# Down products of the second pair of chunks as 2x2 blocks of seven products, one stage behind each gate-up product

## The chip, the core and the metric

One core of a Trainium2 chip runs the whole program. Its engines are TensorE (PE, matrix products; its weight loads are shown as PEld), VectorE (DVE), ScalarE (ACT), GpSimd (POOL) and SyncE (SP, which issues transfers). Each engine runs its own instructions in order; semaphores make one engine wait for another. The metric is device time in microseconds (us), the median of the runs.

## What is computed

One transformer block on 2048 tokens of width 512, in float32: a linear-attention layer with adaptive layer norm, then a gated bilinear layer. The change touches only the second half of the latter, `h @ w_down`.

```python
h = _layernorm(x, axis=-1) * (1 + cb) + sb
g = jnp.einsum("bsd,df->bsf", h, w_gate)      # F = 1376
u = jnp.einsum("bsd,df->bsf", h, w_up)
x = x + gb * jnp.einsum("bsf,fd->bsd", g * u, w_down)
```

## The kernel before

Tokens are cut into four chunks of 512, each chunk into four token tiles of 128. F is cut into eleven f tiles: ten of 128 and number 10 of 96. To keep float32 accuracy on the fast float32r path of PE, every operand is split in a high part (an ACT cast, `split` L182-184) and a low part (a DVE or POOL subtraction, same helper), and every product is three: high by high, high by low, low by high.

**Gate and up.** Two chunks are treated together, (0, 1) first and (2, 3) second. For each f tile, `block` (L910) makes gate and up for both chunks as a 2x2 block product in seven products instead of eight (the Winograd form of Strassen's scheme). Its seven steps p1, p5, p6, p2, p7, p3, p4 are six PE products of 512 columns each (`times`, L887), into four PSUM banks a, b, c, d. Between them ACT copies banks on (`copy`, L896: a to b after p1, d to SBUF after p5, b to c and to SBUF after p6), and DVE adds and multiplies, so that after p3 and p4 the two tiles of h = gate x up are there, one for each chunk. `block` is a generator: it yields after each step, and callbacks in a table `at` put other work behind a step. These carry the preparation of coming weights: scaling of the down rows by `gb` (DVE, at p6), loads for one f tile ahead of the down rows and two ahead of gate/up (SP, at p7), casts and low parts of the gate/up weights of the next f tile (ACT and POOL, `Right.high` and `Right.lows`, at p7), split of the down rows (at p3), and differences of gate/up weights (POOL, `Right.sums`, at p4). The split of the two h tiles goes out at the start of the next block (`flush`).

**Down.** The second pair's f tiles are in groups (10, 0, 1), (2, 3, 4), (5, 6, 7), (8, 9). When a group's h tiles are ready, `down_group` (L964) multiplies them with the down rows, 128 tokens by 512 columns, three PE products for each f tile, token tile and chunk, all f tiles of a group summed in one PSUM bank of the four in the pool `ps_acc`. `evac` (L722) adds the bank to x on DVE and, in a chunk's last group, stores x. The groups' products are cut in parts (`cut_at`, L1064), and one part goes out behind each following block, in one run on PE (L1059-1063); those left over come behind the last block (L1068-1071), where the last token tile is made in two halves of 256 columns.

Of the kernel before, what the change touches and what calls it, by code (L numbers as in the profile page):

```python
# [9 lines left out]
F32R = mybir.dt.float32r  # L10
# [4 lines left out]
P = 128  # L15
# [7 lines left out]
def tile_adaln_block(  # L23
# [875 lines left out]
    def split_h(x, n):  # L899
        h, l = B("kh", dt=F32R)[:n], B("kl", dt=F32R)[:n]  # L900
        split(x, h, l)
        return h, l
# [4 lines left out]
        while todo:  # L907
            todo.pop(0)()

    def block(A, R, out, at, aside=False):  # L910


        n, R = R.n, R.of
        a, b, c, d = (x[:n] for x in banks)

        def T2(tag):
            return B(tag)[:n]

# [92 lines left out]

    draws = {}

    def draw_load(n):
        if n < len(steps):
            f0, k = fts[steps[n][1]]
            draws[n] = load(w_down[f0:f0 + k, :], "raw")

    trickle = []

# [6 lines left out]
    free = [False]  # L1027
    parts = []

    def ffn():  # L1030

        first_side, second_side = side, {}
        m = 0
        for g, (cs, fs) in enumerate(groups):
            last = g + 1 == len(groups) or groups[g + 1][0] != cs
            outs, ds = [], []
            A = first_side if cs == (0, 1) else second_side
            for f in fs:
                out = []
                draw = draws.pop(m)  # L1040

                def scale(d=draw):
                    nc.vector.tensor_tensor(d, d, gb[:d.shape[0]], op=ALU.mult)

                at = {"p6": [scale],
                      "p7": [lambda: draw_load(m + 1), lambda: right_load(m + 2), lambda: right_split(m + 1)],
                      "p3": [lambda: ds.append(split_raw(draw, low=nc.gpsimd))],
                      "p4": [lambda: right_sums(m + 2)]}
                for point in ("p1", "p5", "p6", "p3", "p4")[2 if m == 2 else 0:]:
                    at.setdefault(point, []).append(lambda: some(some_at.get(m, 0)))  # L1050
                if m + 1 < len(steps) and steps[m + 1][0] != cs:
                    at["p1"].append(lambda: fetch(stash, second_side, "a11", "s1"))
                    at["p7"].insert(0, lambda: fetch(stash, second_side, "s2", "a12", "s3"))
                elif m and steps[m - 1][0] != cs:
                    at["p1"].append(lambda: fetch(stash, second_side, "s4", "a22"))
                outs.append(out)
                yield from block(A, rights[m], out, at, aside=not free[0])
# [6 lines left out]
            cut_at = {2: ([[0, 1, 2, 3], []], [[], [0, 1, 2, 3]]),  # L1064
                      3: ([[0, 1, 2], []], [[3], [0, 1]], [[], [2, 3]])}[len((groups + groups[-1:])[g + 1][1])]
# [199 lines left out]
```

## Time and profile before

| | |
|---|---|
| median of 3 runs | 566.18 us (565.63 to 566.36) |
| the profiled execution | 565.84 us |
| its span, first to last instruction | 564.1 us |
| mean granted TensorE clock | 0.999 |
| eleven blocks of the second pair and what follows | from about 384 us to the end |

The profile's page shows the span with the busy time of each engine, the chain of work that ended last, and groups of equal instructions with their count, busy time, mean duration and the idle time in front of them with what ended it. Consecutive instructions of an engine overlap, PE's most of all, so that the time of a run of them is read from their starts. In a timeline each row has the start, the time, the engine, the line, operation, tiles and the count; square brackets show how long the engine sat idle and what released it.

### The profile page before, as it was taken

How to read it: one execution, taken by the hardware profiler on the slowest of the kernel's cores; microseconds unless marked ns; L12 is line 12 of the kernel's file. 1: busy time of each engine (PE TensorE's matmuls, PEld its weight loads, DVE VectorE, ACT ScalarE, POOL GpSimd, SP SyncE). 2: the span in 40 equal slices, each digit the busy share in tenths (PEclk: the TensorE clock that was granted, in tenths of full speed). 3: DMA queues.
4: the chain of work that ended last, by engine and by line, in shares of the span. 5: the costliest groups of instructions: out<-in, count | busy, mean ns of one | idle time of the engine just before them, and what ended most of it. 6: DMA issues, size and time to landing. Idle time of an engine off the chain costs nothing.

```text
span 564.1 us, 7356 instructions
## 1 busy us (share of the span) xinstructions
PE 556.8 (99%) x2568; PEld 457.1 (81%) x2568; DVE 377.4 (67%) x622; ACT 278.5 (49%) x499; POOL 187.0 (33%) x192
## 2 busy tenths in 40 slices
PE   7999999999999999999999999999999999999997
PEld 6788888888888778878878888887888888888886
DVE  7996968868869876759768877756444444344445
ACT  3695866446556546355875454534333333334120
POOL 2000000000011300000598756555667446446200
PEclk9999999999999999999999999999999999999999
DMA  8900224202301001804408363599336022200004
GB/s 286 380 5 2 74 76 131 94 0 72 83 2 57 19 1 38 260 0 150 131 2 295 116 206 112 184 350 310 113 112 189 17 57 56 57 19 2 0 1 149
DMA packets 50309, 59.34 MB, mean 105 GB/s; under 512 B 6432, under 2 KB 27168, under 8 KB 50272
## 3 DMA queue, kind: packets, MB, share of 16 engines
q1 hardware_dynamic: 50272, 58.87, 32.8%
q8 instruction: 20, 0.33, 0.2%
q14 instruction: 17, 0.14, 0.1%
HBM read 43.12 MB, written 15.73 MB: 104 GB/s over the span
## 4 chain that ended last, share of the span: by engine, by line
PE 92%; ACT 2%; DVE 2%; POOL 1%; issue 1%; DMA 1%; SPq 0%; POOLq 0%
PE bank L892 28%; PE acc L972 6%; PE acc L973 6%; PE acc L974 6%; PE acc L662 6%; PE bank L196 5%; PE bank L198 5%; PE bank L197 5%; PE acc L325 3%; PE acc L323 3%; PE acc L324 3%; PE bank L741 2%; PE bank L739 2%; PE bank L740 2%; PE bank L246 2%; PE bank L626 1%
## 5 line engine op out<-in xcount | busy, mean ns | idle before, releaser
L892 PE MATMUL bank<-h,w 128*128 128x512 f32 (+1 forms) x798 | 184.6, 390 | 0.0
L892 PEld LDWEIGHTS bank<-h,w 128*128 128x128 f32 (+1 forms) x798 | 148.4, 186 | 32.4
L897 ACT ACTIVATE bank<-bank 128x512 f32<-128x512 f32 (+1 forms) x38 | 22.1, 582 | 142.9 <-PE bank L892 142.9
L726 DVE TENSOR_TENSOR x<-acc,x 128x512 f32<-128x512 f32 (+1 forms) x73 | 48.9, 683 | 47.5 <-PE acc L974 46.7
L878 POOL TENSOR_TENSOR w<-raw,w 128x256 fp32r<-128x256 f32 (+3 forms) x38 | 42.4, 1115 | 103.0 <-ACT w L871 76.1
L184 POOL TENSOR_TENSOR w<-raw,w 128x512 fp32r<-128x512 f32 (+1 forms) x25 | 34.9, 1401 | 116.0 <-DVE mv L216 87.5
L972 PE MATMUL acc<-w,kh 128*128 128x512 f32 (+2 forms) x154 | 59.6, 387 | 0.0
L973 PE MATMUL acc<-w,kh 128*128 128x512 f32 (+2 forms) x154 | 59.6, 387 | 0.0
L974 PE MATMUL acc<-w,kl 128*128 128x512 f32 (+2 forms) x154 | 59.5, 386 | 0.0
L224 POOL TENSOR_TENSOR rstd<-ve,half 128x4 f32<-128x4 f32 (+1 forms) x10 | 10.6, 1061 | 123.2 <-DVE ve L223 121.6
L184 DVE TENSOR_TENSOR kl<-u,kh 128x512 fp32r<-128x512 f32 (+1 forms) x38 | 27.4, 761 | 31.8 <-ACT kh L183 28.0
L878 POOL TENSOR_TENSOR w<-t,w 128x512 fp32r<-128x512 f32 (+1 forms) x38 | 48.4, 1296 | 0.0
L196 PE MATMUL bank<-w,h 128*128 128x512 f32 x104 | 41.7, 401 | 0.0
L198 PE MATMUL bank<-w,h 128*128 128x512 f32 x104 | 40.6, 390 | 0.0
L197 PE MATMUL bank<-w,h 128*128 128x512 f32 x104 | 40.5, 389 | 0.0
L662 PE MATMUL acc<-w,xh 128*128 128x512 f32 x120 | 38.1, 399 | 0.0
L972 PEld LDWEIGHTS acc<-w,kh 128*128 128x128 f32 (+1 forms) x154 | 28.9, 188 | 6.0
L974 PEld LDWEIGHTS acc<-w,kl 128*128 128x128 f32 (+1 forms) x154 | 28.9, 188 | 5.9
L973 PEld LDWEIGHTS acc<-w,kh 128*128 128x128 f32 (+1 forms) x154 | 28.9, 188 | 5.9
L951 DVE TENSOR_TENSOR u<-bank,u 128x512 f32<-128x512 f32 (+1 forms) x19 | 13.1, 692 | 30.3 <-PE bank L892 26.8
L233 ACT ACTIVATE n<-x,nmr,rstd 128x512 f32<-128x512 f32 x30 | 22.7, 804 | 16.0 <-DVE nmr L227 16.0
L183 ACT ACTIVATE w<-raw 128x512 fp32r<-128x512 f32 (+2 forms) x44 | 26.2, 619 | 2.8 <-DMA raw<-in_A_wqkv_dram 1.9
(188 smaller groups left out, 1108.8 us busy)
## 6 DMA issues: line engine op xcount, KB each, us to landing
raw<-in_w_mod_dram SPq DMA_DIRECT2D x24, 256.0 KB, 3.8
raw<-in_B_w_down_dram SPq DMA_DIRECT2D x20, 256.0 KB, 3.4
raw<-in_B_w_gate_dram SPq DMA_DIRECT2D x36, 128.0 KB, 3.9
raw<-in_B_w_up_dram SPq DMA_DIRECT2D x36, 128.0 KB, 3.9
x<-in_A_x_dram SPq DMA_DIRECT2D x16, 256.0 KB, 5.8
kept<-f SPq DMA_DIRECT2D x16, 256.0 KB, 2.0
f<-kept SPq DMA_DIRECT2D x16, 256.0 KB, 4.3
side_s<-h SPq DMA_DIRECT2D x16, 256.0 KB, 2.5
```

What stands on the lines that cost most here:

```text
L183: nc.scalar.activation(h, src, AF.Copy)
L184: (low or nc.vector).tensor_tensor(l, src, f32(h), op=ALU.subtract)
L196: nc.tensor.matmul(ps, ah, bh, start=i == 0, stop=False)
L197: nc.tensor.matmul(ps, ah, bl, start=False, stop=False)
L198: nc.tensor.matmul(ps, al, bh, start=False, stop=i == n - 1)
L662: nc.tensor.matmul(yps[i], x, y, start=False, stop=k == KD - 1 and x is al, skip_group_check=True)
L726: nc.vector.tensor_tensor(xt[:, a:b], dn[j][:, a:b], xt[:, a:b], op=ALU.add)
L878: sub = lambda out, x, y: (on or nc.gpsimd).tensor_tensor(out, x, f32(y), op=ALU.subtract)
L892: mm = lambda x, y, **kw: nc.tensor.matmul(ps, x[:, k], y, skip_group_check=True, **kw)
L972: nc.tensor.matmul(ps, hh[:, a:b], dh[:n, c:d], start=i == 0, stop=False)
L973: nc.tensor.matmul(ps, hh[:, a:b], dl[:n, c:d], start=False, stop=False)
L974: nc.tensor.matmul(ps, hl[:, a:b], dh[:n, c:d], start=False, stop=i == len(hs) - 1)
```

## The change

The blocks of gate and up stay as they are. In the second pair, the down products of f tiles 0 to 7 are taken in pairs of f tiles, and each pair as a 2x2 block product by the same scheme: rows are the two chunks, inner blocks the two f tiles, columns the two halves of 256 output columns. A new class `Quad` holds one pair. Its left blocks are the four h tiles and four sums of them (DVE, `sum`; `split` makes high and low parts), its right blocks the quarters of the scaled down rows and four differences (POOL, `sums`), with four casts (ACT, `high`) and four low parts (POOL, `lows`).

`stages` makes the seven products for two token tiles at a time: six PE products of 256 columns per stage. It uses three of the four banks of `ps_acc` for the whole time: one bank for each token tile (its two halves hold p1 with p2 and p5 with p3) and a third whose halves are seeded with copies of p1 (ACT) and collect p6, p7 and p4. DVE adds to x after p5, p6, p7, p3 and p4. A pair has fourteen stages; each is put behind one gate-up product, and they run from the second step of the block two f tiles after the pair's first one.

The callbacks of a pair are spread over three blocks: scaling at p6 and p2 and the differences at p3 of the first; the split of a11, then s3, its split, the casts and the low parts at p1 and p5 of the second; s1, s2, s4 and the remaining splits at p1 to p7 of the third, in which the pair's stages begin and the next pair's scaling and differences stand as well. F tiles 10, 8 and 9 keep the plain down products, all behind the last block. The first pair of chunks is computed as before.

```diff
-    def block(A, R, out, at, aside=False):
+    def block(A, R, take_h, at, aside=False):
...
         def mul(ps, x):
             nc.vector.tensor_tensor(x, ps, x, op=ALU.mult)
-            todo.append(lambda: out.append(split_h(x, n)))
+            take_h(x, n)
...
+    class Quad:
+        DH = D // 2
+        ORDER = ("p1", "p5", "p6", "p2", "p7", "p3", "p4")
+        TERMS = {"p1": ("a11", "b11"), "p5": ("s1", "t1"), "p6": ("s2", "t2"), "p2": ("a12", "b21"),
+                 "p7": ("s3", "t3"), "p3": ("s4", "b22"), "p4": ("a22", "t4")}
+        SUMS = {"s1": ("a21", "a22", ALU.add), "s2": ("s1", "a11", ALU.subtract),
+                "s3": ("a11", "a21", ALU.subtract), "s4": ("a12", "s2", ALU.subtract)}
+        def __init__(self, cs):
+            self.cs = cs
+            self.h, self.left, self.right = {}, {}, {}
+            self.raws = []
+            self.names = ["a11", "a21", "a12", "a22"]
+        def take(self, x, n):
+            self.h[self.names.pop(0)] = x
+        def sum(self, n):
+            x, y, alu = self.SUMS[n]
+            self.h[n] = B("s")
+            nc.vector.tensor_tensor(self.h[n], self.h[x], self.h[y], op=alu)
+        def split(self, *names):
+            for n in names:
+                self.left[n] = split_h(self.h[n], P)
+        def sums(self):
+            d1, d2 = (d.rearrange("p (c n) -> p c n", c=2) for d in self.raws)
+            sub = lambda out, x, y: nc.gpsimd.tensor_tensor(out, x, y, op=ALU.subtract)
+            self.t12, self.t34 = (B("t", (P, 2, self.DH)) for _ in range(2))
+            sub(self.t12[:, 0], d1[:, 1], d1[:, 0])
+            sub(self.t12[:, 1], d2[:, 1], self.t12[:, 0])
+            sub(self.t34[:, 0], d2[:, 1], d1[:, 1])
+            sub(self.t34[:, 1], d2[:, 0], self.t12[:, 1])
+        def high(self):
+            d1, d2 = (d.rearrange("p (c n) -> p c n", c=2) for d in self.raws)
+            self.b11 = B("w", (P, 2, self.DH), F32R)
+            nc.scalar.activation(self.b11[:, 0], d1[:, 0], AF.Copy)
+            self.parts = []
+            for names, x in ((("t1", "t2"), self.t12), (("b21", "b22"), d2), (("t3", "t4"), self.t34)):
+                h = B("w", (P, 2, self.DH), F32R)
+                nc.scalar.activation(h, x, AF.Copy)
+                self.parts.append((names, x, h))
+        def lows(self):
+            sub = lambda out, x, y: nc.gpsimd.tensor_tensor(out, x, f32(y), op=ALU.subtract)
+            d1 = self.raws[0].rearrange("p (c n) -> p c n", c=2)
+            self.right["b11"] = (self.b11[:, 0], self.b11[:, 1])
+            sub(self.b11[:, 1], d1[:, 0], self.b11[:, 0])
+            for names, x, h in self.parts:
+                l = B("w", (P, 2, self.DH), F32R)
+                sub(l, x, h)
+                for i, n in enumerate(names):
+                    self.right[n] = (h[:, i], l[:, i])
+        def mm(self, ps, name, j, fresh=False):
+            left, right = self.TERMS[name]
+            (ah, al), (bh, bl) = (tuple(x[:, j * P:(j + 1) * P] for x in self.left[left]), self.right[right])
+            for n, (x, y) in enumerate(((ah, bh), (ah, bl), (al, bh))):
+                nc.tensor.matmul(ps, x, y, start=fresh and n == 0, stop=n == 2, skip_group_check=True)
+        def stages(self, own, seeded, js):
+            N = self.DH
+            x0, x1 = ([xts[c][j] for j in js] for c in self.cs)
+            def add(x, ps):
+                nc.vector.tensor_tensor(x, ps, x, op=ALU.add)
+            for name in self.ORDER:
+                for i, j in enumerate(js):
+                    u, d = own[i][:, :N], own[i][:, N:]
+                    self.mm({"p1": u, "p2": u, "p5": d, "p3": d}.get(name, seeded[i]), name, j, name == "p1")
+                for i, j in enumerate(js):
+                    if name == "p1":
+                        copy(seeded[i], own[i][:, :N])
+                    elif name == "p5":
+                        add(x1[i][:, N:], own[i][:, N:])
+                    elif name == "p6":
+                        add(x0[i][:, N:], seeded[i])
+                    elif name == "p7":
+                        add(x1[i][:, N:], seeded[i])
+                    elif name == "p3":
+                        add(x0[i], own[i])
+                    elif name == "p4":
+                        add(x1[i][:, :N], seeded[i])
+                yield
+        def run(self, banks):
+            own, seed = banks[:2], banks[2]
+            N = self.DH
+            for js in ((0, 1), (2, 3)):
+                yield from self.stages(own, (seed[:, :N], seed[:, N:]), js)
...
-    groups += [((2, 3), g) for g in ((10, 0, 1), (2, 3, 4), (5, 6, 7), (8, 9))]
     steps = [(cs, f) for cs, g in groups for f in g]
+    tail = (10, 8, 9)
+    steps += [((2, 3), f) for f in (10, 0, 1, 2, 3, 4, 5, 6, 7, 8, 9)]
+    M2 = len(steps) - 11
...
+    def plain_h(out):
+        return lambda x, n: todo.append(lambda: out.append(split_h(x, n)))
...
+    def scaled(d):
+        nc.vector.tensor_tensor(d, d, gb[:d.shape[0]], op=ALU.mult)
+    def plain_down(m, at, ds):
+        draw = draws.pop(m)
+        at["p6"].insert(0, lambda: scaled(draw))
+        at["p3"].insert(0, lambda: ds.append(split_raw(draw, low=nc.gpsimd)))
...
+        cs = (2, 3)
+        tail_h, tail_d = [], []
+        hold, running = [], []
+        quads = {}
+        late = {}
+        for n in range(4):
+            quads[m + 1 + 2 * n] = Quad(cs)
+        def advance():
+            while running and next(running[0], True):
+                running.pop(0)
...
+            if f in tail:
+                out = []
+                tail_h.append(out)
+                plain_down(m, at, tail_d)
+                take_h = plain_h(out)
+            elif m in quads:
+                q = quads[m]
+                take_h = q.take
+                for point in ("p6", "p2"):
+                    at[point].append(lambda n=point == "p2": scaled(q.raws[n]))
+                at["p3"].append(q.sums)
+                late[m + 1] = {"p1": [lambda q=q: q.split("a11")],
+                               "p5": [lambda q=q: q.sum("s3"), lambda q=q: q.split("s3"), q.high, q.lows]}
+                late[m + 2] = {"p1": [lambda q=q: q.sum("s1"), lambda q=q: q.split("s1")],
+                               "p5": [lambda q=q: q.sum("s2"), lambda q=q: q.split("s2")],
+                               "p6": [lambda q=q: q.split("a12"), lambda q=q: q.sum("s4")],
+                               "p2": [lambda q=q: q.split("s4")],
+                               "p7": [lambda q=q: q.split("a22")]}
+            if m + 1 in quads:
+                q1 = quads[m + 1]
+                at["p7"].insert(0, lambda: q1.raws.extend(draw_of(n) for n in (m + 1, m + 2)))
+            elif m + 1 < len(steps) and steps[m + 1][1] in tail:
+                at["p7"].insert(0, lambda: draw_load(m + 1))
+            if m - 2 in quads:
+                if not hold:
+                    hold.extend(acc_bank() for _ in range(3))
+                    nc.tensor.matmul(hold[2], wp[0][0][:, :P], wp[0][0], start=True, stop=True)
+                fresh = quads[m - 2].run(hold)
+            for n, _ in enumerate(block(second_side, rights[m], take_h, at)):
+                if n == 1 and m - 2 in quads:
+                    running.append(fresh)
+                advance()
+                yield
+            m += 1
+            if parts:
+                takes = [down_group(*p) for p in parts.pop(0)]
+                yield
+                for take in takes:
+                    take()
         flush()
-        while parts:
-            group = parts.pop(0)
-            for p in group:
-                down_group(*p, by_tile=not parts, end=not parts and p is group[-1])()
+        while running:
+            advance()
+        hold.clear()
+        for i, ch in enumerate(cs):
+            down_group(ch, i, [0, 1, 2, 3], tail_h, tail_d, True, by_tile=True, end=ch == cs[-1])()
```

More of the change, by code (lines that the diff above doesn't have):

```diff
@@ L1012, in tile_adaln_block, with draw_of @@
     draws = {}
+    def draw_of(n):
+        f0, k = fts[steps[n][1]]
+        return load(w_down[f0:f0 + k, :], "raw")
     def draw_load(n):
-        if n < len(steps):
-            f0, k = fts[steps[n][1]]
-            draws[n] = load(w_down[f0:f0 + k, :], "raw")
+        draws[n] = draw_of(n)
     trickle = []
@@ L1028, in tile_adaln_block, with base_points @@
     parts = []
+    def plain_h(out):
+        return lambda x, n: todo.append(lambda: out.append(split_h(x, n)))
+    def base_points(m):
+        cs = steps[m][0]
+        at = {p: [] for p in ("p1", "p5", "p6", "p2", "p7", "p3", "p4")}
+        at["p7"] += [lambda: right_load(m + 2), lambda: right_split(m + 1)]
+        at["p4"].append(lambda: right_sums(m + 2))
+        for point in ("p1", "p5", "p6", "p3", "p4")[2 if m == 2 else 0:]:
+            at[point].append(lambda: some(some_at.get(m, 0)))
+        if m + 1 < len(steps) and steps[m + 1][0] != cs:
+            at["p1"].append(lambda: fetch(stash, second_side, "a11", "s1"))
+            at["p7"].insert(0, lambda: fetch(stash, second_side, "s2", "a12", "s3"))
+        elif m and steps[m - 1][0] != cs:
+            at["p1"].append(lambda: fetch(stash, second_side, "s4", "a22"))
+        return at
@@ L1030, in ffn @@
+    def scaled(d):
[4 more added lines that the diff above has]
+        at["p3"].insert(0, lambda: ds.append(split_raw(draw, low=nc.gpsimd)))
+    second_side = {}
     def ffn():
-        first_side, second_side = side, {}
         m = 0
         for g, (cs, fs) in enumerate(groups):
-            last = g + 1 == len(groups) or groups[g + 1][0] != cs
+            last = g + 1 == len(groups)
@@ L1036, in ffn @@
             outs, ds = [], []
-            A = first_side if cs == (0, 1) else second_side
             for f in fs:
                 out = []
[L1040 to L1055, printed above, removed]
+                at = base_points(m)
@@ L1056, in ffn @@
+                plain_down(m, at, ds)
+                at["p7"].insert(1 if m == M2 - 1 else 0, lambda: draw_load(m + 1))
                 outs.append(out)
-                yield from block(A, rights[m], out, at, aside=not free[0])
+                yield from block(side, rights[m], plain_h(out), at, aside=not free[0])
                 m += 1
@@ L1063, in ffn @@
                         take()
-            cut_at = {2: ([[0, 1, 2, 3], []], [[], [0, 1, 2, 3]]),
-                      3: ([[0, 1, 2], []], [[3], [0, 1]], [[], [2, 3]])}[len((groups + groups[-1:])[g + 1][1])]
+            cut_at = ([[0, 1, 2], []], [[3], [0, 1]], [[], [2, 3]]) if last else ([[0, 1, 2, 3], []], [[], [0, 1, 2, 3]])
             parts.extend([(ch, i, js, outs, ds, last) for i, (ch, js) in enumerate(zip(cs, jss)) if js] for jss in cut_at)
-        flush()
-        while parts:
-            group = parts.pop(0)
-            for p in group:
-                down_group(*p, by_tile=not parts, end=not parts and p is group[-1])()
+        cs = (2, 3)
@@ new lines, in ffn @@
+        tail_h, tail_d = [], []
[7 more added lines that the diff above has]
+                running.pop(0)
+        while m < len(steps):
+            f = steps[m][1]
+            at = base_points(m)
+            for point, dos in late.pop(m, {}).items():
+                at[point] = dos + at[point]
+            if f in tail:
[37 more added lines that the diff above has]
+                    take()
```

## The prediction

> **What bounds the kernel now.** I read the page's busy shares and its chain first, then busy time by stretch, then the timeline of each engine in the second pair of chunks.
>
> ```profile
> PE 556.8 (99%) x2568; PEld 457.1 (81%) x2568; DVE 377.4 (67%) x622; ACT 278.5 (49%) x499; POOL 187.0 (33%) x192
> PE 92%; ACT 2%; DVE 2%; POOL 1%; issue 1%; DMA 1%; SPq 0%; POOLq 0%
> ...
> PE acc L143 <- DVE w L138: 2.0, 1, 2.0
> ...
> core 0: us, PE busy (x) PEld busy (x) DVE busy (x) ACT busy (x) POOL busy (x), PEclk, DMA share, GB/s
> 421.00:541.00 120.00, 120.00 (x530) 99.26 (x529) 51.73 (x80) 42.89 (x84) 63.48 (x66) 1.00 0.17 47
> ```
>
> PE is busy throughout and 92% of the chain; its longest wait is 2.0 us, at the start. In the 120 us where the second pair runs, PE never stops, at full granted clock, while DVE is at 43%, ACT 36%, POOL 53%, DMA 17%. Fewer PE columns are worth their whole time here, as long as nothing makes PE wait.
>
> **PE's own price.** Busy overlaps, so I count starts.
>
> ```profile
> 364.11 0.39 PE L972 MATMUL acc<-w,kh 128*128 128x512 f32 x1
> ...
> 369.55 9.68 PE L892 MATMUL bank<-h,w 128*128 128x512 f32 x42
> 379.07 0.39 PE L972 MATMUL acc<-w,kh 128*128 128x512 f32 x1
> ...
> 558.95 0.28 PE L972 MATMUL acc<-w,kh 128*128 128x256 f32 x1
> ...
> 560.02 0.28 PE L972 MATMUL acc<-w,kh 128*128 128x256 f32 x1
> ```
>
> Twenty-four down products of 512 columns take 369.55 - 364.11 = 5.44, 0.227 each; the 42 of a gate-up block 9.52. The tail has the new shape already: nine starts of 256 columns in 1.07, 0.119 each, 5% over half. Removed: 8 f tiles x 24 x 0.227 = 43.5. Added: 4 pairs x 7 stages x 4 token tiles x 3 = 336 x 0.119 = 40.0, a product that opens the third bank (0.2), and about 0.03 because the split last token tile now sums three f tiles. PE alone: **-3.3 us**. The work after PE's last product (add, store) is unchanged.
>
> **What is put beside PE.** The rows for each kind:
>
> ```profile
> L726 DVE TENSOR_TENSOR x<-acc,x 128x512 f32<-128x512 f32 x22 | 15.1, 692 | 28.2 <-PE acc L974 28.2
> L726 DVE TENSOR_TENSOR x<-acc,x 128x256 f32<-128x256 f32 x2 | 0.8, 425 | 0.3 <-PE acc L974 0.3
> 547.59 2.73 DVE L726 TENSOR_TENSOR x<-acc,x 128x512 f32<-128x512 f32 x4 [5.40 <-PE acc L974]
> 534.59 1.29 DVE L184 TENSOR_TENSOR kl<-u,kh 128x512 fp32r<-128x512 f32 x2 [1.95 <-ACT kh L183]
> 535.80 0.68 DVE L1043 TENSOR_TENSOR raw<-raw,row 128x512 f32<-128x512 f32 x1
> L183 ACT ACTIVATE kh<-u 128x512 fp32r<-128x512 f32 x16 | 9.1, 622 | 0.0
> 399.90 0.58 ACT L897 ACTIVATE bank<-bank 128x512 f32<-128x512 f32 x1 [7.01 <-PE bank L892]
> 402.57 0.58 ACT L897 ACTIVATE bank<-bank 128x512 f32<-128x512 f32 x1 [0.55 <-PE bank L892]
> 403.06 0.59 ACT L897 ACTIVATE u<-bank 128x512 f32<-128x512 f32 x1
> 403.54 0.42 ACT L871 ACTIVATE w<-raw 128x256 fp32r<-128x256 f32 x1
> 403.85 1.15 ACT L874 ACTIVATE w<-t 128x512 fp32r<-128x512 f32 x2
> 404.89 0.63 ACT L874 ACTIVATE w<-raw 128x512 fp32r<-128x512 f32 x1
> L878 POOL TENSOR_TENSOR w<-t,w 128x512 fp32r<-128x512 f32 x14 | 17.8, 1293 | 0.0
> L878 POOL TENSOR_TENSOR w<-raw,w 128x256 fp32r<-128x256 f32 x7 | 5.2, 737 | 41.8 <-ACT w L871 41.8
> L860 POOL TENSOR_TENSOR t<-raw,raw 128x256 f32<-128x256 f32 x7 | 5.2, 738 | 0.0
> ```
>
> Consecutive instructions overlap: starts lie 0.68 apart for a DVE add out of PSUM, 0.61 for a DVE operation in SBUF, 0.49 for an ACT copy out of PSUM, 0.52 for a cast of 512, 0.31 for one of 256; a dependent instruction of another engine sees the full duration (0.69, 0.63, 0.42). An ACT copy of 256 columns out of PSUM isn't shown: between 0.31 and 0.49 I take 0.31, its width's row.
>
> Per pair of f tiles (two blocks, about 29 us) DVE gains 16 adds of 256 (0.43) and 4 of 512, 4 sums and 3 low parts, 13.8 us, and loses two thirds of eight adds, 3.6: 43% becomes about 78%. ACT gains 7 casts and 4 seed copies. POOL gains four differences and four low parts and loses two, 3.0 + 4.6 - 2.6 = 5.0 us, 53% to about 70%. The down-weight loads now go out in twos ahead of the four gate/up loads at p7; SP is past them within a block and DMA is at 17%, so nothing. POOL gets to the low parts of the next gate/up weights 10.6 us into the first block; they and the differences end at 10.6 + 4.6 + 3.0 = 18.2, 2.7 into the second block, where ACT casts them at 6.8: free while that margin of 4 us holds, one for one behind it.
>
> **The waits.** These queues run in order, PE's too: behind a stage that waits stand the gate-up products. I walk them block by block. A slot is a gate-up product (1.36) and a stage (0.71), 2.07. PE's last row ends 0.16 after the next start would be; a release adds 0.04.
>
> *Second f tile of a pair (three blocks).* The built order of ACT is: copy of p5, cast of s3, four casts of the next pair's down weights (`high`), then the two copies of the running pair's p1 into the third bank. The running pair's p5 stage waits for both copies, because it writes the other half of the bank that they read. The p5 gate-up product ends at 3.44 of the block; ACT is past its copy at 4.13. DVE, 2.7 late from the block before, does the low part of a11, two p4 adds and the s3 difference until 4.87. So: cast of s3 4.9, four casts (0.31 + 3 x 0.52) until 7.3, copies read out at 7.7 and 8.0. PE reaches that stage at 5.51: it waits **2.2 us**. With no DVE lag the same queue ends at 6.9, still 1.4 late.
>
> *First f tile (two blocks in the steady state).* DVE is free at 1.6: s1 sum 2.3, cast 2.95, low part 3.6, p4 adds 4.4, s2 sum 5.1; ACT casts s2, then the seed copies end at 6.1 and 6.4: p5 was due at 5.51, 0.6 late. ACT then has two gate-up copies before the cast of a12 (7.85); DVE waits for it, and then low a12, s4, a scaling, p5 adds, low s4, a scaling, p6 adds end at 12.65. The p7 stage reuses that bank and was due at 12.35. About **1.0 us** in all. DVE then has six operations of 512 out of PSUM (two gate-up adds, two products, two p3 adds: 4.1), two p7 adds (0.86) and the low part of a22 (0.61): it ends at 18.2, the block at 14.5 + 1.0 = 15.5, which is the 2.7 used above. The first such block has no p4 adds before it (0.5), the last one scaling less (0.6).
>
> *The block before the first stages.* The same casts stand before the copy that frees bank c for the p7 gate-up product: ACT gets there at 7.0, due 5.44: **1.6 us**. The last block has no `high`: nothing.
>
> A restart after a wait is not free:
>
> ```profile
> 30.58 0.69 DVE L315 SCALAR_TENSOR_TENSOR kl<-phi,kh 128x512 fp32r<-128x512 f32 x1 [0.26 <-ACT kh L314]
> ...
> 31.32 0.19 PEld L325 LDWEIGHTS acc<-kl,xh 128*128 128x128 f32 x1 [0.40 <-DVE kl L315]
> 31.33 0.50 PE L325 MATMUL acc<-kl,xh 128*128 128x512 f32 x1
> 31.43 0.19 PEld L323 LDWEIGHTS acc<-kh,xh 128*128 128x128 f32 x1
> 31.66 0.40 PE L323 MATMUL acc<-kh,xh 128*128 128x512 f32 x1
> ```
>
> The next start comes 0.33 later, not 0.23: 0.1 for each of some twelve waits, 1.2.
>
> **Sum:** -3.3 + 3 x 2.2 + 2 x 1.0 + 0.5 + 0.6 + 1.6 + 1.2 = +9.2. The profiled execution took 565.84 (span 564.1 and 1.7 around it), 0.3 under the median of 566.18: 565.84 + 9.2 = **575.0 us**.
>
> By the Trainium skill ("PSUM — Partial Sum Buffer", "PSUM bank collisions raise a hardware error") two engines must not touch one bank at once even in disjoint columns, so waits go by bank; the built waits agree, and no run here shows a collision. If waits went by half banks instead, the copies would be due one slot later, at the p6 stage: 0.4 instead of 2.2 three times, and the sum would give 569.6.
>
> **The rivals.**
>
> *DVE keeps up, only ACT's queue is late.* The three blocks cost 1.4 and the one before about 1.0, with four restarts: -3.3 + 4.2 + 1.0 + 0.4 = +2.3, 568.1. For it: DVE idled 57% of the stretch. Against it: the chains sum, cast, low part cross two engines four times in one block.
>
> *No overlap of starts.* If every operation holds its engine for its full duration (0.58 to 0.69), the same walk gives 2.9 for the second tiles, 1.9 for the two first ones (1.5 and 0.9 at the ends), 2.3 before: waits of 17.2 instead of 11.3, 580.9. For it: where engines wait on each other the overlap is lost. Against it: the rows of starts above.
>
> *The casts hide (the other side).* ACT sits idle up to 7.01 us for PE (the row at 399.90). If `high` and the seed copies pass in such a gap, PE only loses columns: -3.3, 562.5. It is decided in the second tile's p5 slot: what ACT has queued there must take under 2.07. Against it: that queue is 3.4 us by the rows, and its place is fixed in the order.
>
> *The clock drops.* At the start of the kernel, after PE's idle 2.0 us, products are slower:
>
> ```profile
> 2.00 6.86 PE L143 MATMUL acc<-w 128*128 128x512 f32 x20 [2.00 <-DVE w L138]
> 9.86 0.65 PE L253 MATMUL bank<-ident,n 128*128 128x128 f32 x4 [1.00 <-ACT n L233]
> 10.28 0.71 PE L143 MATMUL acc<-w 128*128 128x512 f32 x2
> ```
>
> Twenty at 0.227 would take 4.7; the start costs 2.16 more. After four waits near 2 us that would add 8.6: 583.6. Against it: at 9.86 PE had waited 1.0, and the two products at 10.28 took 0.71, near their 0.62; the new waits hardly reach 2.3.
> By the Trainium skill ("TensorE: Matmul & The Clock Gate", "What's actually happening") the clock halves after an idle window of about 3.4 us, so these gaps alone would not do it; no run here shows a gap of that length amid work.
>
> **How the numbers follow.** The forecast 57% (571 to 579), DVE keeping up 16%, no overlap 11%, the clock 6%, casts hidden 10%. The range 568 to 582 takes in the first three and leaves out the last two and the edges. Within 0.2% of the median is about what a measurement of this kernel can't tell from no change: 565.0 to 567.3. Faster takes 8 of the last case's 10; no change its other 2 and 4 from DVE keeping up; slower is the rest.
>
> **What would show it.** Right: some 336 products of 256 columns at 0.12 apart; PE waits some 10 to 12 us in all; the longest repeat three times at the p5 stage and name ACT's copy, with the four casts right before it on ACT; one wait for ACT's copy into bank c in the block before the stages; DVE near 75 to 80% and PE under 98%. Wrong: PE without waits in this stretch (the casts hide), waits that name DVE most (the chains are longer than the casts), POOL as releaser (its margin was gone), 256-column starts well over 0.12, or a lower granted clock.

## The result, and the profile after

| | before | changed |
|---|---|---|
| median, 6 runs each | 566.27 us (565.63 to 566.66) | 583.88 us (582.28 to 585.45) |
| ratio | | 1.0311, 95% interval 1.0289 to 1.0333 |
| the profiled execution | 565.84 | 585.45 (span 583.7, clock 0.991) |

The change made the kernel 17.6 us slower, 8.9 more than forecast and just outside the range. The busy shares on the page of the changed kernel:

```profile
PE 563.5 (97%) x2716; PEld 464.5 (80%) x2716; DVE 419.2 (72%) x706; ACT 294.8 (51%) x535; POOL 213.3 (37%) x216
```

PE is now idle in 3% of the span. Its list of waits in the changed kernel (total, times, longest) says where:

```profile
PE acc L1056 <- ACT acc L897: 8.5, 4, 2.7
...
PE bank L892 <- DVE u L920: 1.9, 3, 0.6
PE bank L892 <- ACT bank L897: 1.6, 1, 1.6
PE acc L1056 <- DVE x L1066: 1.0, 3, 0.3
```

Three waits near 2.7 are for the seed copies, at the p5 stage of the second f tiles, as forecast; the 1.6 in the block before is as forecast too. The three of 0.6 for a product on DVE (L920), at the first gate-up product of each second f tile, stand in no step of the forecast. The stretch block by block (first and second f tile of each pair in turn; busy time with counts, then granted clock, DMA share and GB/s):

```profile
core 0: us, PE busy (x) PEld busy (x) DVE busy (x) ACT busy (x) POOL busy (x), PEclk, DMA share, GB/s
426.59:442.65 16.06, 14.71 (x79) 11.95 (x78) 12.28 (x19) 7.53 (x15) 9.03 (x9) 1.00 0.27 69
442.65:463.16 20.51, 17.86 (x85) 15.24 (x85) 10.58 (x20) 7.70 (x16) 18.03 (x20) 0.83 0.24 69
463.16:479.64 16.48, 15.49 (x86) 12.67 (x85) 13.31 (x23) 7.52 (x15) 5.86 (x5) 1.00 0.04 10
479.64:498.84 19.20, 16.49 (x84) 14.15 (x85) 10.61 (x20) 7.69 (x16) 18.00 (x20) 0.91 0.26 75
498.84:515.34 16.50, 15.49 (x87) 12.70 (x85) 13.33 (x23) 7.52 (x15) 5.87 (x5) 1.00 0.03 10
515.34:533.11 17.77, 15.06 (x84) 12.93 (x85) 10.60 (x20) 7.70 (x16) 17.07 (x19) 1.00 0.22 60
```

The three second f tiles hold the same work and the same waits, yet take 20.51, 19.20 and 17.77: in the first two the clock was 0.83 and 0.91. PE's timeline shows it:

```profile
451.17 0.80 PE L1056 MATMUL acc<-w,kh 128*128 128x256 f32 x2 [2.65 <-ACT acc L897]
...
458.24 0.40 PE L1056 MATMUL acc<-w,kh 128*128 128x256 f32 x2
...
461.06 1.55 PE L892 MATMUL bank<-h,w 128*128 128x512 f32 x6
462.44 0.40 PE L1056 MATMUL acc<-w,kh 128*128 128x256 f32 x2
...
463.16 1.55 PE L892 MATMUL bank<-h,w 128*128 128x512 f32 x6
...
479.64 1.61 PE L892 MATMUL bank<-h,w 128*128 128x512 f32 x6 [0.62 <-DVE u L920]
...
488.16 0.80 PE L1056 MATMUL acc<-w,kh 128*128 128x256 f32 x2 [2.71 <-ACT acc L897]
...
491.85 0.40 PE L1056 MATMUL acc<-w,kh 128*128 128x256 f32 x2
```

A slot, one gate-up product and one stage, takes 463.16 - 461.06 = 2.10 undisturbed. After the wait at 451.17 two slots took 7.07 instead of 4.20, after that at 488.16 one took 3.69: 2.9 + 1.6 = 4.5 us of slow products. Such a spell at half clock is called a drop below. What ACT did before the second of these waits:

```profile
485.34 0.63 ACT L183 ACTIVATE kh<-s 128x512 fp32r<-128x512 f32 x1 [1.35 <-DVE s L1016]
485.88 0.40 ACT L1034 ACTIVATE w<-raw 128x256 fp32r<-128x256 f32 x1
486.19 0.61 ACT L1038 ACTIVATE w<-t 128x512 fp32r<-128x512 f32 x1
486.71 0.61 ACT L1038 ACTIVATE w<-raw 128x512 fp32r<-128x512 f32 x1
487.23 0.61 ACT L1038 ACTIVATE w<-t 128x512 fp32r<-128x512 f32 x1
487.74 0.76 ACT L897 ACTIVATE acc<-acc 128x256 f32<-128x256 f32 x2
```

The order is the forecast one: cast of s3, four casts, seed copies. But ACT sits idle for 1.35 before it, waiting for DVE's s3 sum (1.26 there). DVE and POOL in the changed kernel, at the end of the first f tile:

```profile
473.99 1.24 DVE L1151 TENSOR_TENSOR raw<-raw,row 128x512 f32<-128x512 f32 x1
474.63 2.99 POOL L878 TENSOR_TENSOR w<-t,w 128x512 fp32r<-128x512 f32 x2
...
476.41 1.75 DVE L184 TENSOR_TENSOR kl<-u,kh 128x512 fp32r<-128x512 f32 x1
477.58 1.73 POOL L878 TENSOR_TENSOR w<-raw,w 128x512 fp32r<-128x512 f32 x1
478.09 0.68 DVE L955 TENSOR_TENSOR u<-bank,u 128x512 f32<-128x512 f32 x1
```

The low part of a22 takes 1.75; by the forecast's rows it is 0.69. It ends 0.54 after POOL's pair does (474.63 + 2.99 = 477.62), and POOL's next takes 1.73 and not 1.29. The DVE operation behind it, which reads a PSUM bank, has its usual 0.68.

### The profile page after: what moved, and what is told of

Read it like the earlier page. It is cut to its first block, busy times and chain, and to the rows that moved or that the text cites. A ratio compares the mean times of both kernels' runs of the same rounds, so it can differ in the third digit from the quotient of the medians.

```text
span 583.7 us, 7867 instructions
## 1 busy us (share of the span) xinstructions
PE 563.5 (97%) x2716; PEld 464.5 (80%) x2716; DVE 419.2 (72%) x706; ACT 294.8 (51%) x535; POOL 213.3 (37%) x216
## 5 line engine op out<-in xcount | busy, mean ns | idle before, releaser
L892 PE MATMUL bank<-h,w 128*128 128x512 f32 (+1 forms) x798 | 196.9, 395 | 3.6 <-DVE u L920 1.9
L184 POOL TENSOR_TENSOR w<-raw,w 128x512 fp32r<-128x512 f32 (+1 forms) x17 | 24.6, 1455 | 109.4 <-DVE mv L216 87.5
L1056 PE MATMUL acc<-w,kh 128*128 128x256 f32 x224 | 45.3, 296 | 9.6 <-ACT acc L897 8.5
L1056 PEld LDWEIGHTS acc<-w,kh 128*128 128x128 f32 x224 | 38.7, 197 | 18.1 <-ACT acc L897 11.7
L726 DVE TENSOR_TENSOR x<-acc,x 128x512 f32<-128x512 f32 (+1 forms) x49 | 32.4, 678 | 20.5 <-PE acc L974 19.7
L1066 DVE TENSOR_TENSOR x<-acc,x 128x256 f32<-128x256 f32 (+1 forms) x80 | 34.5, 469 | 17.5 <-PE acc L1056 17.5
L972 PE MATMUL acc<-w,kh 128*128 128x512 f32 (+3 forms) x91 | 34.8, 383 | 0.0
L973 PE MATMUL acc<-w,kh 128*128 128x512 f32 (+3 forms) x91 | 34.8, 383 | 0.0
L974 PE MATMUL acc<-w,kl 128*128 128x512 f32 (+3 forms) x91 | 34.8, 382 | 0.0
L1056 PE MATMUL acc<-w,kl 128*128 128x256 f32 x112 | 32.4, 289 | 0.0
L860 POOL TENSOR_TENSOR t<-raw,t 128x256 f32<-128x256 f32 (+1 forms) x34 | 29.1, 856 | 1.3
```

What stands on the lines that cost most here:

```text
L184: (low or nc.vector).tensor_tensor(l, src, f32(h), op=ALU.subtract)
L892: mm = lambda x, y, **kw: nc.tensor.matmul(ps, x[:, k], y, skip_group_check=True, **kw)
L972: nc.tensor.matmul(ps, hh[:, a:b], dh[:n, c:d], start=i == 0, stop=False)
L973: nc.tensor.matmul(ps, hh[:, a:b], dl[:n, c:d], start=False, stop=False)
L974: nc.tensor.matmul(ps, hl[:, a:b], dh[:n, c:d], start=False, stop=i == len(hs) - 1)
L1056: nc.tensor.matmul(ps, x, y, start=fresh and n == 0, stop=n == 2, skip_group_check=True)
```

## The experiments

Four questions: is it ACT's order that makes the long waits; what does the clock cost, and do the gaps cause it; what stretches DVE; and can the 3.3 us that PE saves be had at all. The kernel before was measured beside each run, at 565.98 to 566.11.

**1. The four casts later.**

```diff
-  "p5": [... q.sum("s3"), ... q.split("s3"), q.high, q.lows]
+  "p5": [... q.sum("s3"), ... q.split("s3")],
+  "p2": [q.high, q.lows]
```

> The four casts and low parts of the next pair's down weights (high, lows) go from point p5 of the second f tile to point p2, behind the two gate-up copies; the cast of s3 stays ahead of the seed copies. Theory A (the order of ACT's queue makes the long waits, and the long waits drop the clock): the four casts are 1.86 us of the 2.9, so the three waits for the seed copies shrink to about 1.0 to 1.2 (the cast of s3 still stands before them), the wait of 1.6 for the copy into bank c goes, and gaps of that length no longer drop the clock: 3 x 1.8 + 1.5 + 4.9 = 11.8 off, about 572. Theory B (DVE's chains are late anyway, and the casts only fill time that ACT would wait): the three waits stay over 2 us and the time at 580 or above. Theory C (the clock drops after any gap of about 1 us): waits shrink as in A, but the clock still drops in two of three, about 577.

Measured: 577.61 us, ratio 1.0204 (1.0188 to 1.0219), clock 0.997 to 1.0. PE's waits:

```profile
PE acc L1056 <- ACT acc L897: 6.4, 7, 1.0
PE bank L892 <- DVE u L920: 1.9, 3, 0.6
PE acc L1056 <- DVE x L1066: 0.9, 3, 0.3
```

The long waits fell to 0.83 or 0.84 and the 1.6 is gone, so the casts did make them. Theory B fell, and C with it: two of the four runs have a clock of 0.997, which is one drop (see run 4), and two have none. The total is still 5.6 above theory A's 572: the p5 stages of the first f tiles, which waited 0.41 once and too little for the list elsewhere, now wait 0.8 to 1.0 each time. A likely reason is that DVE caught up in the long waits; no run tried that apart, so it is not shown.

**2. The s3 sum and its cast later as well.**

```diff
-  "p5": [... q.sum("s3"), ... q.split("s3"), q.high, q.lows]
+  "p2": [... q.sum("s3"), ... q.split("s3"), q.high, q.lows]
```

> As before it, and the sum and split of s3 go to point p2 too, so that on ACT the two seed copies of the running pair stand right behind the copy of p5, which is done 0.1 after the p5 product's next slot begins. Theory A: all three waits and the wait in the block before go to about nothing (under 0.3 each) and the clock stays up: 3 x 2.9 + 1.6 + 4.9 = 15.2 off, about 568.5 to 569. Theory B (DVE late): DVE's adds of the stage before still hold something back; a wait that names DVE appears in the same place and the time stays above 572.

Measured: 572.98 us, ratio 1.0120 (1.0103 to 1.0137), clock 0.999 to 1.0.

```profile
PE acc L1056 <- ACT acc L897: 3.1, 4, 1.2
PE bank L892 <- DVE u L920: 1.9, 3, 0.6
PE acc L1056 <- DVE x L1066: 0.9, 3, 0.3
```

No wait is left at the p5 stage of the second f tiles; the four for ACT are all in first f tiles. With its two orders changed, ACT gives back 10.9 us of the 17.6, the clock's share among it. The time is still 4 us above theory A's: DVE's waits stayed, in other places than theory B had them.

**3. The gaps filled with products.**

```diff
+  if name == "p5" and js[0] and self.followed:
+      for _ in range(11):
+          nc.tensor.matmul(filler, wp[0][0][:, :P], wp[0][0], start=True, stop=True)
```

> The changed kernel, with 11 products of 512 columns (11 x 0.227 = 2.5 us) into the unused fourth bank put in front of the p5 stage in the three blocks that wait there; their result is thrown away. They fill gaps of 2.65 to 2.9 and delay nothing that ACT or DVE do. Theory A (PE's idle gap drops the clock): the windows after the gaps are at full clock, the three waits read 0.1 to 0.4, and the time falls by the price of the drops, 4.9 us in the profiled run, by somewhat less in runs with less of it: about 579 to 580. Rival (the lower clock has another cause than the gap, such as the load that went before): the clock drops as before and the time stays at 583 to 585.

Measured: 580.92 us, ratio 1.0264 (1.0248 to 1.0279); clock 1.0 in three of four runs, 0.999 in one; the three waits are 0.22 or less. PE does more, ACT and DVE the same, and it is faster, if by 0.9 less than expected: the drops come from PE's idle gaps.

**4. Meant to leave out low parts**, by the edit shown in 5, but with the list under the name `second`. That name is bound to something else further down, so no operation was left out: this is the changed kernel once more.

> The changed kernel without the low parts of three of the four gate-up weight operands of each pair's second f tile (the high part is used in their place, so the output lacks these corrections): POOL does not run while DVE makes the low part of a22 at the end of the first f tile. Theory S (a DVE operation whose operands are all in SBUF is slowed while POOL runs one): that low part takes 0.69 instead of 1.75 and the scaling 0.68 instead of 1.24; the waits of 0.62 at the first product of the second f tile go, and the whole DVE queue of these blocks is about 1 us earlier, so the s3 sum and what follows come earlier against PE: the three long waits stay near 2.9 as PE is earlier too; about 3 x 0.6 off, 582. Rival (the operation is long for another reason, such as its place in DVE's queue): it stays at 1.75 and the time does not move.

Measured: 582.97 us (581.30 to 584.00), ratio 1.0295 (1.0272 to 1.0317). It says nothing of theory S, but gives four more runs with their clocks. Sorted, the ten runs of the changed kernel read: 581.30 at clock 1.0; 582.10, 582.28, 582.41 at 0.997; 583.70, 583.84, 584.00, 584.05 at 0.994; 584.95, 585.45 at 0.991. Each 0.003 of clock, which is one drop of 3.41 us at half clock in a span of 581, goes with some 1.3 us. Without a drop the kernel takes about 581.3, so in the median of 583.88 the clock is 2.6.

**5. Low parts left out.**

```diff
+    bare = [M2 + 2 + 2 * i for i in range(4)]
...
-            rights[n].lows(on)
+            rights[n].lows(on, n in bare)
...
-                l = self.tile("w", F32R)
-                sub(l, x, h)
+                l = h
+                if not skip:
+                    l = self.tile("w", F32R)
+                    sub(l, x, h)
```

> The run e4_no_lows left nothing out: the name that held its list of blocks is used again further down, so its L878 rows are all there, and it is a second measurement of the changed kernel (582.97, three waits of 2.70, the low part of a22 at 1.76, the waits of 0.62 as before). This one has the name mended: for the second f tile of each pair three of the four gate-up weight operands get no low part (the high part is used instead), so POOL is idle while DVE makes the low part of a22. Theory S (DVE and POOL slow each other where both work in SBUF): the low part of a22 takes 0.69 instead of 1.75, the scaling 0.68 instead of 1.24, the three waits of 0.62 at the first product of the second f tile go, 3 x (0.6 + 0.25) = 2.5 off: 580.5. POOL's differences also come earlier, so the s3 sum (1.26) may be freed too; the long waits stay at 2.7, as what sets them begins with the p5 product. Rival (those times have another cause): 1.75 stays, the time at 583.

The high part stands where the low part should, so the output of this kernel is not that of the block; it serves for its times alone.

Measured: 579.87 us (578.62, 578.99 at clock 0.994; 580.75, 580.93 at 0.991), ratio 1.0251 (1.0233 to 1.0269). At equal clock that is 5.1 (0.994) and 4.4 (0.991) under the changed kernel. Its waits and two DVE rows:

```profile
PE acc L1058 <- ACT acc L899: 6.0, 4, 1.9
PE bank L894 <- ACT bank L899: 1.6, 1, 1.6
PE acc L1058 <- DVE x L1068: 1.0, 3, 0.3
```

```profile
471.33 0.77 DVE L184 TENSOR_TENSOR kl<-u,kh 128x512 fp32r<-128x512 f32 x1
...
477.83 0.68 DVE L1018 TENSOR_TENSOR s<-u,u 128x512 f32<-128x512 f32 x1
```

The low part of a22 takes 0.77 instead of 1.75, the s3 sum 0.68 and not 1.26; the three waits of 0.6 are gone and the long ones fell from 2.7 to 1.86, which the expectation had denied. The scaling, 1.23, did not fall: POOL's differences now stand beside it. Theory S holds, and it is the largest thing the forecast missed.

**6. Gaps of 2.2.** Two products in place of eleven.

> As e3_fill_gaps, but with 2 products of 512 in front of each of the three p5 stages instead of 11: PE's idle gaps become 2.65 - 0.45 = 2.2, the length that the prediction gave them. Nothing else moves: without a drop of the clock the time is that of e3_fill_gaps, 580.9. If gaps of 2.2 are long enough to drop the clock, it stays near 583. Theory: a gap of 1.6 (block before the first stages) and of 1.0 (e1_casts_late) left the clock at 1.00, 2.65 to 2.71 dropped it in two of three; 2.2 lies between, and I expect no drop, 580.5 to 581.5.

Measured: 581.20 us, ratio 1.0272 (1.0257 to 1.0288), clock 1.0 in three runs, 0.997 in one; waits 2.19 to 2.28. So, as expected, gaps of 2.2 mostly leave the clock alone. But in run 5, whose profile has three gaps of 1.86, it was at 0.994 or 0.991 every time, so length alone doesn't decide. The traces show what parts the cases. In each of them the clock changes only at multiples of 3.413 us after its first rise (in the changed kernel at 450.50, 457.32, 488.04 and 491.46, which lie two, nine and one of these apart). Cut run 5 at such edges, around its first and its second gap (the columns are those of the table by blocks; PEclk is third from the end):

```profile
445.17:448.58 3.41, 1.84 (x10) 1.23 (x9) 1.54 (x3) 2.91 (x7) 1.52 (x2) 1.00 0.00 0
448.58:452.00 3.42, 3.13 (x19) 2.86 (x20) 0.82 (x2) 3.39 (x8) 3.42 (x4) 1.00 0.00 0
479.30:482.72 3.42, 1.56 (x10) 1.27 (x10) 1.22 (x3) 3.39 (x9) 3.15 (x3) 1.00 0.03 7
482.72:486.13 3.41, 3.41 (x13) 2.94 (x12) 0.46 (x2) 1.85 (x5) 3.41 (x5) 0.50 0.00 0
```

The first gap lies across an edge, with 1.57 of its idle time on one side, and the clock stays; the second lies whole between two edges, and the next 3.41 us are at half clock. It is the same wherever the clock was full: the six stretches of 3.41 that a drop follows (two each in the changed kernel and in run 5, one each in runs 4 and 8) have 1.86 to 2.63 us of PE idle; no stretch in any trace here with 1.80 or less has one behind it. That includes the third gap of 2.71 in the changed kernel (1.04 and 1.67) and the gaps of run 6 (1.47 at most). No run moved a gap on purpose, so this is read from the traces and not tested.

**7. The stages two slots later.**

```diff
-                if n == 1 and m - 2 in quads:
+                if n == 3 and m - 2 in quads:
```

with s3 and the casts behind the gate-up casts at p7, and the split of a22 at p4.

> The version that should have no long waits: the stages of a pair start two slots later (beside the p2 product of the first f tile and not the p5 product), so that the seed copies of p1 fall where ACT has no gate-up copies and no s2 to cast; s3 sum and split and the four casts go behind the casts of the next gate-up weights at p7; the split of a22 goes behind the last product at p4. Theory A: no wait over 0.4, clock at full speed; what is left over PE's own -3.3 is the longer slot (2.10 instead of 2.075, 56 times: 1.4) and some 1 to 2 us of small waits: 564.5 to 566.5, the same as before. Theory B (DVE at 75 to 80% cannot keep its chains ahead of PE wherever they are put): waits for DVE of 0.5 to 1 in most blocks, 569 or more.

Measured: 577.99 us, ratio 1.0212 (1.0196 to 1.0227), clock 0.999 to 1.0. Theory A fell, and theory B describes it better: four waits for seed copies, 0.92 to 1.66, and seven for DVE, up to 0.80. Two of the four pairs of copies themselves waited for DVE's adds out of the third bank (0.63 and 0.64); the other two stood behind a cast that had waited for a DVE sum.

**8. The low part of a22 on POOL.**

```diff
-  "p7": [lambda q=q: q.split("a22")]
+  "p7": [lambda q=q: q.split("a22", low=nc.gpsimd)]
```

> The changed kernel with one operation on another engine: the low part of a22, 1.75 us on DVE at the end of the first f tile, goes to POOL (1.29 there), in front of the low parts of the next gate-up weights. Nothing is left out. Theory S (DVE and POOL stretch each other, and that low part in front of the two products is what makes the first product of the second f tile wait): the three waits of 0.62 go, 3 x (0.62 + 0.26) = 2.6, and DVE's s3 sum starts earlier, 1 us of the queue ahead of the long waits; how much of these goes depends on whether the s3 sum still meets POOL's differences, which move back by 1.3: 577 to 580 with one or two drops of the clock in it. Rival (the waits belong to PE's and ACT's order, and DVE only fills time): the waits of 0.62 stay, 583.

Measured: 581.15 us, ratio 1.0275 (1.0260 to 1.0290), clock 0.994 to 0.997: 1.2 under the changed kernel at equal clock (0.997), where 3 to 6 were expected. The waits of 0.62 went, but the time beside POOL moved to the scaling, and with it the wait, to the p7 stage:

```profile
469.97 1.76 POOL L184 TENSOR_TENSOR kl<-u,kh 128x512 fp32r<-128x512 f32 x1 [7.71 <-PE bank L892]
470.50 1.79 DVE L1151 TENSOR_TENSOR raw<-raw,row 128x512 f32<-128x512 f32 x1
...
473.00 0.50 PE L1056 MATMUL acc<-w,kh 128*128 128x256 f32 x2 [0.90 <-DVE x L1066]
```

**9 to 12. Moves on top of run 2**, each for a wait left in the trace before it: s2 to p6, second scaling to p7, low part of a22 on POOL (9); then the first scaling to p2 and the s1 sum to p4 of the block before (10); the s1 sum alone (11); the s1 sum, with the scalings at p7 and p3 (12).

> e2_s3_late with three further moves, each for a wait that is left in its trace: s2's sum and split from p5 to p6, so that the seed copies do not stand behind its cast (waits of 1.17, 0.75, 0.61, 0.61 at the first f tile's p5 stage); the second scaling of a down weight from p2 to p7 (0.31 three times at the p7 stage, for a DVE add); the low part of a22 on POOL (0.62 three times). Theory A: all ten waits go, with their 0.26 each: 572.98 - 5.9 - 2.6 = 564.5, that is PE's own -3.3 and the longer slot, +1.4; 563.5 to 566. Rival (DVE's chains only move: with 72% of the time busy and operations stretched beside POOL's, another wait for DVE takes the place): 567 to 571.

Measured: 567.77 us, ratio 1.0038 (1.0026 to 1.0050). That is the rival's range. Only two listed waits are left in the stretch, 0.9 together; in the middle two pairs three slots of the first f tile take 2.37 to 2.44.

> e9_four_moves still loses some 0.3 at three stages of each first f tile: its s1 sum takes 1.57 beside POOL's differences, which makes the adds of p4, the seed copies and s2 late, and the scaling at p6 stands in front of the adds that free the bank of the p2 stage. Two more moves: the s1 sum goes from p1 to p4 of the block before, in front of the adds of p3; the first scaling goes from p6 to p2, behind the adds of p5. Theory A (each wait has one late DVE operation behind it, and PE's own saving of 3.3 is there to be had): 12 x 0.3 = 3.6 off, 564.2, 1.8 under the kernel before. Rival (DVE's and POOL's shared time only moves on to the next operation): 566.5 to 568.

Measured: 570.26 us, ratio 1.0078 (1.0064 to 1.0092): slower than run 9 and above both expectations. The scaling met POOL's low part, the p6 adds behind it came late, and the p7 stage waited:

```profile
466.30 1.30 POOL L184 TENSOR_TENSOR kl<-u,kh 128x512 fp32r<-128x512 f32 x1 [3.30 <-ACT kh L183]
...
466.34 1.80 DVE L1151 TENSOR_TENSOR raw<-raw,row 128x512 f32<-128x512 f32 x1
...
468.86 0.51 PE L1056 MATMUL acc<-w,kh 128*128 128x256 f32 x2 [0.76 <-DVE x L1066]
```

> Of the two moves that e10_six_moves adds to e9_four_moves, only the s1 sum at p4 of the block before; the scalings stay at p6 and p7. In e10's trace the first scaling met the low part of a22 on POOL and took 1.80, and the adds of p6 behind it made the p7 stage wait 0.75 to 0.84; the s1 sum itself fell from 1.57 to 0.91 to 1.04 and one slot in each first f tile from 2.40 to 2.12. So: e9's 567.77 less 4 x 0.3 = 566.6 if that move is good by itself; 567.8 or more if the sum's time beside POOL's only goes to the low part of s1 behind it (1.00 in e9, 1.27 in e10).

Measured: 567.36 us, ratio 1.0023 (1.0013 to 1.0033), between the two expectations. The s1 sum fell from 1.57 to 1.32, but its low part rose from 1.00 to 1.70, beside POOL, and the three slots take 2.33 to 2.45, as before.

> As e11_s1_early, with both scalings of the next down weights behind the adds that PE waits for: at p7 and p3 of the first f tile in place of p6 and p7. Theory A (each lost 0.3 has one late DVE operation ahead of an add): the slots of the first f tile fall to 2.10, and the time to 564.5 to 565.5, under the kernel before. Rival (the scalings meet POOL's low parts wherever they stand, and now delay the products that free banks a and c): 567 or more, with a wait for u<-bank at L892 in the second f tile.

Measured: 567.50 us, ratio 1.0027 (1.0016 to 1.0039), the rival's time; the wait that it named is not there. The second scaling, now beside POOL, takes 1.71 instead of 1.22; two of the three long slots are shorter (2.17 to 2.21 and 2.08 to 2.10), and a new one of 2.58 to 2.66 with a wait of 0.3 for a DVE add has come. In both runs the shared time moved on. No order tried beats the kernel before; the best, run 11, is 0.23% over it, 16 us under the change as made.

## Why the prediction was wrong

Its sum against the profiled execution of the changed kernel. A listed wait costs 0.26 more than its number, by the forecast's own 0.16 and 0.1.

| term | forecast | measured, and from what |
|---|---|---|
| PE's products | -3.3 | -3.3 by their count |
| longer slot | 0 | 1.5: 56 x (2.10 - 2.074), with 2.074 from six products of each kind at the forecast's prices |
| block before the stages | 1.7 | 1.9: 1.60 + 0.26 |
| long waits, second f tiles | 6.9 | 8.9: 2.65 + 2.71 + 2.71 + 3 x 0.26 |
| p5 and p7 stages, first f tiles | 3.9 | 2.4: 0.41 + 0.97 + 4 x 0.26 |
| first product, second f tiles | 0 | 2.6: 1.85 + 3 x 0.26 |
| clock | 0 | 4.5 |
| sum | 9.2 | 18.5, of 19.6; the rest is in stalls too short for the list |

- **ACT's order: right.** Place, releaser and the four casts before the copies are as forecast, and runs 1 and 2 show that they cause the waits.
- **The step that failed first** is the price of a DVE operation in SBUF: "0.61 for a DVE operation in SBUF", "a dependent instruction of another engine sees the full duration (0.69, 0.63, 0.42)", and beside it POOL's 5 us more counted as a queue alone, "free while that margin of 4 us holds". The quoted rows, at 534.59 and 535.80, and the like in the nine blocks before them, fall into moments in which POOL did nothing. By run 5 the stretch is 4.4 to 5.1 us: it lengthened the long waits by 0.8 each and made the waits of 0.62. With it gone the long waits are 1.86, or 2.1 with their 0.26, against the forecast's 2.3. The trace of before had the warning, in the first pair of chunks and in the first block of the second:

```profile
304.73 1.74 POOL L878 TENSOR_TENSOR w<-raw,w 128x512 fp32r<-128x512 f32 x1
305.25 1.77 DVE L184 TENSOR_TENSOR h<-f,h 128x512 fp32r<-128x512 f32 x1
306.44 1.73 POOL L184 TENSOR_TENSOR w<-raw,w 128x512 fp32r<-128x512 f32 x1
...
387.29 2.15 DVE L184 TENSOR_TENSOR kl<-u,kh 128x512 fp32r<-128x512 f32 x2 [1.88 <-ACT kh L183]
```

The row at 305.25 is a low part of the same form as those at 0.69, at 1.77, with POOL at work on both sides of it. The row at 387.29 is the same pair of low parts as the one that the prediction quoted at 534.59, some blocks earlier: there it took 1.29, and here, with POOL at work, 2.15. The Trainium skill ("SBUF — State Buffer", "SBUF: two separate sides") states it as a rule: a DVE operation with both inputs in SBUF and a GpSimd one that reads SBUF take turns, and the later one waits for the whole of the earlier. The traces agree. In run 10 POOL's low part at 466.30 started first and kept its 1.30, and DVE's scaling, 0.04 behind it, took 1.80. In the changed kernel each waited for the one before it (1.75 and 1.73), while DVE's reads of PSUM keep their 0.68. The prediction did not weigh that rule.
- **The clock: the wrong rival taken.** It stood at 6%, because "the new waits hardly reach 2.3". They reached 2.7, and 1.86 was enough in run 5, where a gap lay whole between two of the clock's edges. Its 583.6 lies 0.3 from the median, but by luck: it set four drops of 2.16 on the forecast's 575.0, where the clock is 2.6 of the median and the stretch of DVE's and POOL's operations, 4.4 to 5.1, is the larger part. The sentence drawn from the Trainium skill ("TensorE: Matmul & The Clock Gate", "What's actually happening"), that gaps of this length would not do it, is not borne out. The same section says that its window runs on by itself and that results vary from run to run; the clocks of 1.0 to 0.991 in runs of one kernel, and the edges found in run 6, agree with that.
- **The slot: a small size off.** Products of 512 and of 256 columns were priced from rows in which each kind follows its own; where six of 512 columns and six of 256 take turns, a slot is 2.10.
- **The p5 and p7 stages of the first f tiles: too dear** (3.9 against 2.4), while the long waits stand; with these cut, run 1, they grow.
- **The other rivals.** "DVE keeps up" fell with DVE's waits in every run. "No overlap of starts" gave 580.9, beside the 581.3 without a drop, but the starts do overlap where POOL is idle, so the near number is luck. "The casts hide" fell: they stood in front of the copies three times.

That the removed columns are worth little here is shown by run 11: with no listed wait but two in the stretch, it is still not under the kernel before. The slot of 2.10 takes back 1.5 of the 3.3, and slots over 2.10 take 3.7 in its trace. At two of them, in the pair at 458 us, the weight loads wait for the seed copies (0.35), which had waited for DVE's adds (0.97), and for a DVE low part (0.24).

## What to carry to other kernels

Price an operation in SBUF with the other engine at work that will be at work beside it: look for the longest case of the same form in the trace, not only for the nearest one. A gap in PE can have a second price behind it, in the clock, that differs from run to run; compare runs of equal clock before other causes are weighed. And where a change saves 3 us of PE but gives DVE a chain of sums, casts and low parts for every stage, the order of the other engines' queues is the change: here, with one operation moved to POOL and the drops of the clock gone with the gaps, it was worth 16 us, five times the saving.

## What was not expected of the hardware

- DVE and POOL operations in SBUF stretch each other: 0.69 to 1.75 or 1.80 on DVE, 1.29 to 1.76 on POOL. The one that starts first keeps its time (POOL's 1.30 in run 10), the other waits for it.
- The granted clock fell after gaps of 2.65 to 2.71 in two of three cases of one execution, in all four executions of run 5 (1.86 in its profile), and in one of four of run 6 (2.19 to 2.28 in its profile). In every trace here it fell after a stretch of 3.41 us, counted from the clock's first rise, with at least 1.86 of PE idle in it, and after none with 1.80 or less.
